# Lightning attention into a gated FFN: block 0's masks, k transposes and first outputs reordered, block 1's first transposes moved behind a gate

## The chip, the cores and the metric

One core of one Trainium2 chip. The metric is the device time of one execution in microseconds. All runs here were of the fast state, at a granted clock of 0.998 to 1.0, but for two executions at 0.992. A profile covers a span about 2.1 us shorter than that time (224.5 of 226.6 us for the kernel before).

## The reference

Causal linear attention with decay over blocks, then a gated FFN. Shapes: q, k, v (4, 8, 768, 64), d_model 512, d_ff 1536, float32 in and out.

```python
for b in range(nb):                                   # blocks along the sequence
    intra = einsum('bhic,bhjc->bhij', qb, kb) * Dmask # scores, decay mask
    intra = einsum('bhij,bhjd->bhid', intra, vb)      # output within the block
    inter = einsum('bhid,bhde->bhie', qb * lam_pow, kv_state)
    out[:, :, sl] = intra + inter
    kv_state = lam_block * kv_state + einsum('bhsd,bhse->bhde', kb * rev_pow, vb)
# x: (3072, 512)
gate = 1 / (1 + exp(-(x @ w_gate))); val = x @ w_val
return gate * val @ w_out
```

## The kernel before

It works in six blocks of 128 positions, all four batches (b0 to b3) together. In block 0 there is no state yet: q and k are turned on the matrix engine (PE), q is scaled (QS), k is copied (KS), scores (`piece_s`) are multiplied by a mask on the vector engine (DVE, `piece_m` gives MT), and MT times V gives the output (`piece_a0`), which the scalar engine (ACT) copies to XT. The FFN runs in 12 units of 128 columns, each a gate product, a value product and a multiplication; `gv(0, 8)` is unit 8 of block 0. While block 0's FFN runs, block 1's attention is slipped in between. All loads but those of q of b0 and b1 and of the decay factors go through Pool's queue in the order of the program.

The start, with cuts marked:

```python
    idle(10)                       # fillers: PE has nothing yet
    nc.vector.tensor_copy(Q[0][:, 0], q01[0])
    piece_tq0([0]); make_mask(0); idle(1)
    piece_tq0([1]); piece_tk0(0); make_mask(1); idle(1)
    piece_s(0, [0]); piece_m(0, 0); piece_s(0, [1]); piece_m(0, 1, (0,))
    piece_tk0(1)                   # k of b2, copy, k of b3, copy: one PSUM tile
    # ... (table load)
    piece_tq0([2]); piece_tq0([3]); piece_m(0, 1, (1,))
    piece_s(0, [2], ps_ff, "ff"); piece_m(0, 2)
    piece_s(0, [3]); piece_m(0, 3)
    make_kd0(0, nc.vector)         # decayed k for the state
    piece_a0(0); piece_a0(1); idle(2)
    piece_a0(2, (nc.scalar.copy, nc.scalar.copy))
    g0 = psum(); mm_part(g0, WG, 0, 0, 0, 3 * C)     # "first gate": b0 to b2
    v0 = psum(); mm_part(v0, WV, 0, 0, 0, 3 * C)
    piece_a0(3, (nc.scalar.copy, nc.vector.tensor_copy))
    make_kd0(1, nc.vector); c(0, 0)                  # state of b0, b1
    mm_part(g0, WG, 0, 0, 3 * C, TCH); sigm(0, 0, g0)   # "full gate": b3
    # ... unit 0's rest, unit 1, c(0, 1), units 2 to 8 ...
    gv(0, 8)
    t(1, 0)                        # turn q and k of block 1 (b0, b1), scale q, copy k
    gv(0, 9)
    sc(1, 0)                       # scores of block 1
```

Of the kernel before, what the change touches and what calls it, by code (L numbers as in the profile page):

```python
# [8 lines left out]
BF16 = mybir.dt.bfloat16  # L9
# [6 lines left out]
def kernel(  # L16
# [11 lines left out]
    nc = tc.nc  # L28

    B, H, S, D = q.shape  # L30
    C = 128
    NSTEP = S // C
    HP = H // 2
# [4 lines left out]
    TCH = B * C  # L38
# [5 lines left out]
    trsb = ctx.enter_context(tc.tile_pool(name="trsb", bufs=3))  # L44
# [6 lines left out]
    ps_at = ctx.enter_context(tc.tile_pool(name="ps_at", bufs=5, space=bass.MemoryType.PSUM))  # L51
    ps_ff = ctx.enter_context(tc.tile_pool(name="ps_ff", bufs=3, space=bass.MemoryType.PSUM))
# [8 lines left out]
    WG = const.tile([128, NMT, DFF], BF16, tag="WG")  # L61
    WV = const.tile([128, NMT, DFF], BF16, tag="WV")
# [5 lines left out]
    Q, K, V = {}, {}, {}  # L68
# [42 lines left out]
    nc.scalar.preload_act_table_set("natural_log_exp_and_others")  # L111
    ident = const.tile([128, 128], BF16, tag="ident")
    zero = const.tile([128, TCH], BF16, tag="zero")
    jn = const.tile([128, 2], FP32, tag="jn")
    ip1 = const.tile([128, C], FP32, tag="ip1")
    tri = const.tile([128, C], FP32, tag="tri")
    nc.vector.memset(zero, 0.0)
    Sb = stp.tile([128, B, HP, D], BF16, tag="Sb", name="Sb")
    nc.vector.memset(ip1[:, 0:1], 1.0)
    w = 1  # L120
# [30 lines left out]
    def idle(n):  # L151
        for i in range(n):
            nc.tensor.matmul(wm, lhsT=zero[:, :C], rhs=zero, start=True, stop=True,
                             skip_group_check=True)
# [40 lines left out]
    def make_mask(u):  # L195
        nc.vector.tensor_tensor(
            out=mask[:, u::2, :], in0=tri.unsqueeze(1).to_broadcast([128, HP, C]),
            in1=pk[:, u::2].unsqueeze(2).to_broadcast([128, HP, C]), op=ALU.mult)

    def masked(out, x, n, u):  # L200
        if n == 0:
            nc.vector.tensor_tensor(out=out, in0=x, in1=mask[:, u::2, :], op=ALU.mult)
            return
        nc.vector.tensor_tensor(  # L204
            out=out.rearrange("p (e x) c -> p e x c", e=2), in0=x.rearrange("p (e x) c -> p e x c", e=2),
            in1=mask.rearrange("p (x u e) c -> p u e x c", u=2, e=2)[:, u], op=ALU.mult)
# [7 lines left out]
    QS, KS, MT, XT, KD = {}, {}, {}, {}, {}  # L214

    QR, HB = {}, {}
# [20 lines left out]
    def transpose_pair(out, x, b, g):  # L237
        nc.tensor.transpose(out, x[:, b, 2 * g:2 * g + 2, :].rearrange("p h d -> p (h d)"), ident)  # L238

    def scale(n, bp, src):  # L240
        QS[n, bp] = trsb.tile([128, 2, 2, 2, C], BF16, tag="QS", name="QS")
        nc.vector.tensor_tensor(out=QS[n, bp].rearrange("p e i x c -> p e i (x c)"),
                                in0=src.rearrange("p e i x c -> p e i (x c)"),
                                in1=lamq_e.unsqueeze(2).to_broadcast([128, 2, 2, 2 * C]), op=ALU.mult)

    def piece_tq0(bs, then=None):
        tq = ps_at.tile([128, 2, 2, 2 * C], BF16, name="tq", tag="ps")
        for b in bs:
            if (0, b // 2) not in QS:
                QS[0, b // 2] = trsb.tile([128, 2, 2, 2, C], BF16, tag="QS", name="QS")  # L250
            for g in range(HP):
                transpose_pair(tq[:, b % 2, g // 2, g % 2 * C:g % 2 * C + C], Q[0], b, g)
        if then:
            then()
        for b in bs:
            nc.vector.tensor_tensor(out=QS[0, b // 2][:, :, b % 2].rearrange("p e x c -> p e (x c)"),
                                    in0=tq[:, b % 2], in1=lamq0_e, op=ALU.mult)

    def piece_tk0(bp):
        KS[0, bp] = trsb.tile([128, 2, 2, 2, C], BF16, tag="KS", name="KS")  # L260
        for i in range(2):
            if i == 0 or bp == 0:
                tk = ps_at.tile([128, 1 + bp, 2, 2 * C], BF16, name="tk", tag="ps")
            x = tk[:, i if bp else 0]
            for g in range(HP):
                transpose_pair(x[:, g // 2, g % 2 * C:g % 2 * C + C], K[0], 2 * bp + i, g)
            nc.scalar.copy(KS[0, bp][:, :, i].rearrange("p e x c -> p e (x c)"), x)  # L267

    def piece_t(n, bp):
        if n > 1 or bp == 1:  # L270
            scale(n, bp, QR[n][:, :, 2 * bp:2 * bp + 2] if n > 1 else HB["q"])
            return
        q1, k1 = (x[1][:, 0].rearrange("p (e b y d) -> p e b y d", e=2, b=2, y=HP) for x in (Q, K))
        tq = ps_at.tile([128, 2, 2, 2, C], BF16, name="tq", tag="ps")
        tk = ps_at.tile([128, 2, 2, 2, C], BF16, name="tk", tag="ps")

        def turn(out, x):
            for e in range(2):
                for i in range(2):
                    for g in range(2):  # L280
                        nc.tensor.transpose(out[:, e, i, g, :],
                                            x[:, e, i, 2 * g:2 * g + 2, :].rearrange("p y d -> p (y d)"), ident)

        turn(tq, q1)
        scale(n, bp, tq)
        turn(tk, k1)
        KS[n, bp] = trsb.tile([128, 2, 2, 2, C], BF16, tag="KS", name="KS")
        nc.scalar.copy(KS[n, bp], tk)

    SP = {}  # L290

    def piece_s(n, bs, pool=ps_at, tag="ps"):

        for b in bs:
            bp, i = b // 2, b % 2
            sp = [pool.tile([128, HP, C], FP32, name=f"sp{u}", tag=tag) for u in range(2)]
            for hp in range(HP):
                for u in range(2):
                    us = slice(u * 64, (u + 1) * 64)
                    nc.tensor.matmul(sp[u][:, hp, :], lhsT=KS[n, bp][us, hp // 2, i, hp % 2, :],  # L300
                                     rhs=QS[n, bp][us, hp // 2, i, hp % 2, :],
                                     start=(hp == 0), stop=(hp == HP - 1), skip_group_check=True)
            SP[n, b] = sp

    def piece_m(n, b, us=(0, 1)):
        if us[0] == 0:
            MT[n, b] = mtp.tile([128, 2, HP, C], BF16, tag="MT", name="MT")
        for u in us:
            masked(MT[n, b][:, u], SP[n, b][u], n, u)
# [32 lines left out]
    def piece_a0(b, split=()):  # L342
        if 0 not in XT:
            XT[0] = xtp.tile([128, NMT, B, C], BF16, tag="XT", name="XT")
        w = 2 if split else NMT
        for m0 in range(0, NMT, w):
            pool, tag = (ps_ff, "ff") if b == 2 and m0 else (ps_at, "ps")
            op = pool.tile([128, w, C], FP32, name="op", tag=tag)
            for m in range(w):
                intra(0, b, op[:, m, :], m0 + m, m == 0, m == w - 1)  # L350
            cp = split[m0 // w] if split else nc.scalar.copy
            cp(XT[0][:, m0:m0 + w, b, :], op)  # L352
# [78 lines left out]
    def mm_part(ps, W, n, ft, lo, hi):  # L431
        x = XT[n].rearrange("p m b c -> p m (b c)")
        for mt in range(NMT):
            nc.tensor.matmul(ps[:, lo:hi], lhsT=W[:, mt, ft * 128:(ft + 1) * 128], rhs=x[:, mt, lo:hi],  # L434
                             start=(mt == 0), stop=(mt == NMT - 1))

    def psum():
        return ps_ff.tile([128, TCH], FP32, name="gp", tag="ff")

    def sigm(n, ft, gp):  # L440
        HT[n, ft] = htp.tile([128, TCH], BF16, tag="sg", name="sg", bufs=3)
        nc.scalar.activation(HT[n, ft], gp, AF.Sigmoid)

    def prod(n, ft, vp):
        sg = HT[n, ft]
        HT[n, ft] = htp.tile([128, TCH], BF16, tag="ht", name="ht", bufs=2 * NFT)
        nc.vector.tensor_mul(HT[n, ft], sg, vp)
# [52 lines left out]
    nc.vector.tensor_copy(Q[0][:, 0], q01[0])  # L500
    piece_tq0([0])
    make_mask(0)
    idle(1)
    piece_tq0([1])
    piece_tk0(0)
    make_mask(1)
    idle(1)
    piece_s(0, [0])
    piece_m(0, 0)
    piece_s(0, [1])  # L510
    piece_m(0, 1, (0,))
    piece_tk0(1)
    nc.scalar.preload_act_table_set("sigmoid_and_others")
    piece_tq0([2])
    piece_tq0([3])
    piece_m(0, 1, (1,))
    piece_s(0, [2], ps_ff, "ff")
    piece_m(0, 2)
    piece_s(0, [3])
    piece_m(0, 3)  # L520
    make_kd0(0, nc.vector)
    piece_a0(0)
    piece_a0(1)
    idle(2)
    piece_a0(2, (nc.scalar.copy, nc.scalar.copy))
    g0 = psum()
    mm_part(g0, WG, 0, 0, 0, 3 * C)
# [18 lines left out]
    def t(n, bp):  # L546
        piece_t(n, bp)

    def sc(n, bp):
        piece_s(n, [2 * bp, 2 * bp + 1])  # L550
        piece_m(n, 2 * bp)
# [7 lines left out]
    def gv(n, *fts):  # L559
        for ft in fts:  # L560
            piece_gv(n, ft)
# [36 lines left out]
    lamq_end()  # L598
    gv(0, 6, 7)
    gv(0, 8)  # L600
    t(1, 0)
    gv(0, 9)
    sc(1, 0)
    m(1, 0)
    gv(0, 10)
# [101 lines left out]
```

## Time and profile before

| | |
|---|---|
| time, three runs | 226.60 us (226.56 to 226.66) |
| PE idle, 0 to 20 us | 3.8 of 20.0 us |
| PE idle, 20 to 191 us | 0.04 us |
| DMA engines busy, 5.6 to 40 us | 90% or more in every slice of the page |

PE's order is the kernel's time: from 20 us to the tail it never waits by the view of waits, so whatever starts it earlier ends the kernel earlier, unless something else is late. (That view misses stalls that the modelled ends of matmuls cover.) And the DMA engines are busy without a break in the stretch where PE starts. The sums come from the view of busy time by stretches (PE busy 3.81 + 2.17 + 2.71 + 3.62 + 3.90 in 0 to 20 us).

### The profile page before, as it was taken

The page shows a single profiled execution, that of the slowest core. Times are in us where ns is not written, and L with a number is a line of the kernel's source. Part 1 is how long each engine was busy: PE and PEld are TensorE (multiplying, and loading weights), DVE is VectorE, ACT ScalarE, POOL GpSimd, SP SyncE. Part 2 cuts the span into 40 slices and gives each one's busy share as a digit, 9 for nine tenths or more (in the row PEclk, how much of TensorE's full clock was granted, in tenths as well). Part 3 has the DMA queues.
Part 4 walks back from the last instruction along what each step waited for, and adds up shares of the span by engine and source line. Part 5 has one row for each costly group of instructions (what it writes and reads, how often), then busy time and mean ns, then how long its engine had stood idle before and what let it go on. Part 6 is the DMA issues. An engine that isn't in the chain of part 4 may idle for free.

```text
span 224.5 us, 4262 instructions
## 1 busy us (share of the span) xinstructions
PE 217.8 (97%) x1746; PEld 114.7 (51%) x1746; DVE 105.8 (47%) x192; ACT 79.8 (36%) x151; POOL 79.2 (35%) x78
## 2 busy tenths in 40 slices
PE   7689999999999999999999999999999999999994
PEld 2454455888854454444445444446444445444443
DVE  7797747595521713336732445742335840333300
ACT  5564334435422234333225333115333225333221
POOL 8996698983592008930006940000000000000000
PEclk9999999999999999999999999999999999999999
DMA  6999999999999992999021999021930012100022
GB/s 109 155 169 193 191 176 155 163 183 168 157 162 159 225 236 86 210 157 101 1 96 55 231 151 128 0 96 47 168 70 0 0 52 91 47 3 0 0 93 95
DMA packets 106419, 25.70 MB, mean 114 GB/s; under 512 B 97056, under 2 KB 103456, under 8 KB 106400
## 3 DMA queue, kind: packets, MB, share of 16 engines
q0 software_dynamic: 81792, 13.90, 81.6%
q1 hardware_dynamic: 23568, 11.28, 20.4%
q10 hardware_dynamic: 1040, 0.26, 0.5%
q8 instruction: 13, 0.21, 0.4%
q14 instruction: 6, 0.05, 0.1%
HBM read 28.32 MB, written 6.29 MB: 154 GB/s over the span
## 4 chain that ended last, share of the span: by engine, by line
PE 94%; DMA 3%; ACT 1%; issue 1%; DVE 0%; POOLq 0%
PE po L483 27%; PE gp L420 21%; PE vp L426 21%; PE gp L455 5%; PE gp L434 5%; PE vp L461 5%; PE sp L300 3%; PE op L313 3%; DMA kb<-in_k_dram 3%; PE op L325 1%; PE po L472 1%; PE cp L404 1%; ACT KS L267 1%; PE tk L238 1%; ACT XT L352 0%
## 5 line engine op out<-in xcount | busy, mean ns | idle before, releaser
L429 DVE TENSOR_TENSOR ht<-sg,vp 128x512 bf16<-128x512 bf16 x54 | 37.1, 687 | 64.2 <-PE vp L426 64.0
L483 PE MATMUL po<-WO,ht 128*128 128x512 bf16 x276 | 62.0, 379 | 0.0
L420 PE MATMUL gp<-XT,WG 128*128 128x512 bf16 x216 | 55.5, 379 | 0.0
L426 PE MATMUL vp<-XT,WV 128*128 128x512 bf16 x216 | 55.4, 379 | 0.0
L423 ACT ACTIVATE sg<-gp 128x512 bf16<-128x512 f32 x54 | 32.2, 597 | 59.0 <-PE gp L420 59.0
L483 PEld LDWEIGHTS <-ht 128*128 128x128 bf16 x276 | 26.3, 98 | 31.0
L426 PEld LDWEIGHTS <-WV 128*128 128x128 bf16 x216 | 21.2, 98 | 25.5
L420 PEld LDWEIGHTS <-WG 128*128 128x128 bf16 x216 | 20.8, 98 | 24.7
L486 ACT COPY ob<-po 128x512 f32<-128x512 f32 x23 | 13.5, 586 | 52.2 <-PE po L483 50.4
L204 DVE TENSOR_TENSOR MT<-sp,mask 128x512 bf16<-128x512 f32 x40 | 25.1, 682 | 9.1 <-PE sp L300 9.1
L382 POOL TENSOR_TENSOR sd<-Sb,dec 128x512 f32<-128x512 bf16 x8 | 8.1, 1037 | 41.2 <-DVE Sb L411 41.1
L455 PE MATMUL gp<-XT,WG 128*128 128x256 bf16 x96 | 14.4, 273 | 0.0
L461 PE MATMUL vp<-XT,WV 128*128 128x256 bf16 x96 | 14.4, 273 | 0.0
L465 DVE TENSOR_TENSOR ht<-sg,vp 128x256 bf16<-128x256 bf16 x24 | 10.0, 420 | 8.6 <-PE vp L461 8.6
L458 ACT ACTIVATE sg<-gp 128x256 bf16<-128x256 f32 x24 | 9.2, 384 | 13.0 <-PE gp L455 11.8
L91 POOL DMA_DIRECT2D vb<-in_v_dram x10 | 12.7, 1278 | 1.0 <-DMA WG<-in_moe_w_gate_dram 0.6
L373 POOL TENSOR_TENSOR kd<-kb,kds 128x1024 bf16<-128x1024 bf16 x6 | 11.3, 1904 | 4.7 <-PE vp L461 4.7
L411 DVE TENSOR_TENSOR Sb<-cp,sd 128x512 bf16<-128x512 f32 x8 | 5.2, 686 | 15.5 <-PE cp L404 15.5
L340 ACT CAST XT<-op 128x512 bf16<-128x512 f32 x19 | 9.9, 598 | 2.1 <-PE op L313 2.0
L455 PEld LDWEIGHTS <-WG 128*128 128x128 bf16 x96 | 9.2, 98 | 1.7 <-issue 0.2
L461 PEld LDWEIGHTS <-WV 128*128 128x128 bf16 x96 | 9.4, 98 | 1.1
L77 POOL DMA_DIRECT2D qb<-in_q_dram x8 | 9.4, 1182 | 0.0
(79 smaller groups left out, 162.1 us busy)
## 6 DMA issues: line engine op xcount, KB each, us to landing
out_dram<-ob SPq DMA_DIRECT2D x21, 256.0 KB, 2.0
kb<-in_k_dram POOLq DMA_DIRECT2D x10, 256.0 KB, 8.4
qb<-in_q_dram POOLq DMA_DIRECT2D x8, 256.0 KB, 8.1
vb<-in_v_dram POOLq DMA_DIRECT2D x4, 512.0 KB, 13.7
WO<-in_moe_w_out_dram POOLq DMA_DIRECT2D x3, 512.0 KB, 8.7
WV<-in_moe_w_val_dram POOLq DMA_DIRECT2D x5, 256.0 KB, 8.8
WG<-in_moe_w_gate_dram POOLq DMA_DIRECT2D x4, 256.0 KB, 8.6
qb<-in_q_dram POOLq DMA_DIRECT2D x6, 128.0 KB, 8.3
```

The costliest lines, as they stand in the source:

```text
L91: nc.gpsimd.dma_start(out=lst[n][:, b0:b1], in_=src[b0:b1, :, sl, :].rearrange("b h s d -> s (b h) d"))
L204: nc.vector.tensor_tensor(out=out.rearrange("p (e x) c -> p e x c", e=2), in0=x.rearrange("p (e x) c -> p e x c", e=2), in1=mask.rearrange ...
L373: nc.gpsimd.tensor_tensor(out=KD[n][:, e], in0=K[n][:, e], in1=kds[:, e::2].unsqueeze(1).unsqueeze(3).to_broadcast([128, B, HP, D]), op=AL ...
L420: nc.tensor.matmul(gp, lhsT=WG[:, mt, fs], rhs=x[:, mt, :], start=(mt == 0), stop=(mt == NMT - 1))
L423: nc.scalar.activation(sg, gp, AF.Sigmoid)
L426: nc.tensor.matmul(vp, lhsT=WV[:, mt, fs], rhs=x[:, mt, :], start=(mt == 0), stop=(mt == NMT - 1))
L429: nc.vector.tensor_mul(HT[n, ft], sg, vp)
L434: nc.tensor.matmul(ps[:, lo:hi], lhsT=W[:, mt, ft * 128:(ft + 1) * 128], rhs=x[:, mt, lo:hi], start=(mt == 0), stop=(mt == NMT - 1))
L455: nc.tensor.matmul(gp[:, cs], lhsT=WG[:, mt, fs], rhs=x[:, mt, cs], start=(mt == 0), stop=(mt == NMT - 1))
L461: nc.tensor.matmul(vp[:, cs], lhsT=WV[:, mt, fs], rhs=x[:, mt, cs], start=(mt == 0), stop=(mt == NMT - 1))
L483: nc.tensor.matmul(po, lhsT=HT[n, ft][:, tt * 128:(tt + 1) * 128], rhs=WO[:, ft, :], start=(ft == 0), stop=(ft == NFT - 1))
L486: nc.scalar.copy(ob, po)
```

## The change

Its intent: shorten the way from k's landing to the first FFN product by giving DVE a better order and taking a wait out of k's transposes; put b0's and b1's outputs in PE's pauses; and turn block 1's k later, when it has surely landed.

```diff
-    def piece_tk0(bp): # transposes of one batch, its copy, then the next, in one tile
+    def piece_tk0(*bs):
+        ...
+        for j, b in enumerate(bs):        # all transposes
+            ...
+        for j, b in enumerate(bs):        # then all copies
+            nc.scalar.copy(KS[0, bp]..., tk[:, j])
@@ start
     make_mask(0)
+    make_mask(1)
     idle(1)
     piece_tq0([1])
     piece_tk0(0)
-    make_mask(1)
+    piece_tk0(1)
 ...
-    piece_tk0(1)
+    piece_tk0(2, 3)
     piece_tq0([2])
-    piece_tq0([3])
     piece_m(0, 1, (1,))
-    piece_s(0, [2], ps_ff, "ff")
-    piece_m(0, 2)
+    def first():
+        piece_s(0, [2], ps_ff, "ff")
+        piece_m(0, 2, (0,))
+    piece_tq0([3], first)                 # first() before q of b3 is scaled
+    piece_m(0, 2, (1,))
+    piece_a0(0)
+    piece_a0(1)
     piece_s(0, [3])
     piece_m(0, 3)
     make_kd0(0, nc.vector)
-    piece_a0(0)
-    piece_a0(1)
-    idle(2)
     piece_a0(2, (nc.scalar.copy, nc.scalar.copy))
@@ block 1
-    t(1, 0)
-    gv(0, 9)
+    g9 = psum(); mm_part(g9, WG, 0, 9, 0, TCH); sigm(0, 9, g9)
+    scale(1, 0, turn(Q, (0, 1)))
+    for e, cp in enumerate((nc.scalar.copy, nc.vector.tensor_copy)):
+        cp(KS[1, 0][:, e:e + 1], turn(K, (e,)))   # half on ACT, half on DVE
+    v9 = psum(); mm_part(v9, WV, 0, 9, 0, TCH); prod(0, 9, v9)
```

(The zero memset also moves up past three tile declarations.)

More of the change, by code (lines that the diff above doesn't have):

```diff
@@ L113 @@
     zero = const.tile([128, TCH], BF16, tag="zero")
+    nc.vector.memset(zero, 0.0)
     jn = const.tile([128, 2], FP32, tag="jn")
@@ L116 @@
     tri = const.tile([128, C], FP32, tag="tri")
-    nc.vector.memset(zero, 0.0)
     Sb = stp.tile([128, B, HP, D], BF16, tag="Sb", name="Sb")
@@ L257, in piece_tq0 @@
                                     in0=tq[:, b % 2], in1=lamq0_e, op=ALU.mult)
-    def piece_tk0(bp):
-        KS[0, bp] = trsb.tile([128, 2, 2, 2, C], BF16, tag="KS", name="KS")
-        for i in range(2):
-            if i == 0 or bp == 0:
-                tk = ps_at.tile([128, 1 + bp, 2, 2 * C], BF16, name="tk", tag="ps")
-            x = tk[:, i if bp else 0]
+    def piece_tk0(*bs):
+        bp = bs[0] // 2
+        if (0, bp) not in KS:
+            KS[0, bp] = trsb.tile([128, 2, 2, 2, C], BF16, tag="KS", name="KS")
+        tk = ps_at.tile([128, len(bs), 2, 2 * C], BF16, name="tk", tag="ps")
+        for j, b in enumerate(bs):
@@ L265, in piece_tk0 @@
             for g in range(HP):
-                transpose_pair(x[:, g // 2, g % 2 * C:g % 2 * C + C], K[0], 2 * bp + i, g)
-            nc.scalar.copy(KS[0, bp][:, :, i].rearrange("p e x c -> p e (x c)"), x)
+                transpose_pair(tk[:, j, g // 2, g % 2 * C:g % 2 * C + C], K[0], b, g)
+        for j, b in enumerate(bs):
+            nc.scalar.copy(KS[0, bp][:, :, b % 2].rearrange("p e x c -> p e (x c)"), tk[:, j])
     def piece_t(n, bp):
-        if n > 1 or bp == 1:
-            scale(n, bp, QR[n][:, :, 2 * bp:2 * bp + 2] if n > 1 else HB["q"])
-            return
@@ L273, in piece_t @@
-        q1, k1 = (x[1][:, 0].rearrange("p (e b y d) -> p e b y d", e=2, b=2, y=HP) for x in (Q, K))
-        tq = ps_at.tile([128, 2, 2, 2, C], BF16, name="tq", tag="ps")
-        tk = ps_at.tile([128, 2, 2, 2, C], BF16, name="tk", tag="ps")
-        def turn(out, x):
-            for e in range(2):
-                for i in range(2):
-                    for g in range(2):
-                        nc.tensor.transpose(out[:, e, i, g, :],
-                                            x[:, e, i, 2 * g:2 * g + 2, :].rearrange("p y d -> p (y d)"), ident)
@@ L284, in piece_t, with turn @@
-        turn(tq, q1)
-        scale(n, bp, tq)
-        turn(tk, k1)
-        KS[n, bp] = trsb.tile([128, 2, 2, 2, C], BF16, tag="KS", name="KS")
-        nc.scalar.copy(KS[n, bp], tk)
+        scale(n, bp, QR[n][:, :, 2 * bp:2 * bp + 2] if n > 1 else HB["q"])
+    def turn(x, es):
+        x = x[1][:, 0].rearrange("p (e b y d) -> p e b y d", e=2, b=2, y=HP)
+        out = ps_at.tile([128, len(es), 2, 2, C], BF16, name="tq", tag="ps")
+        for j, e in enumerate(es):
+            for i in range(2):
+                for g in range(2):
+                    nc.tensor.transpose(out[:, j, i, g, :],
+                                        x[:, e, i, 2 * g:2 * g + 2, :].rearrange("p y d -> p (y d)"), ident)
+        return out
@@ L600 @@
     gv(0, 8)
-    t(1, 0)
-    gv(0, 9)
+    g9 = psum()
+    mm_part(g9, WG, 0, 9, 0, TCH)
+    sigm(0, 9, g9)
+    scale(1, 0, turn(Q, (0, 1)))
+    KS[1, 0] = trsb.tile([128, 2, 2, 2, C], BF16, tag="KS", name="KS")
+    for e, cp in enumerate((nc.scalar.copy, nc.vector.tensor_copy)):
+        cp(KS[1, 0][:, e:e + 1], turn(K, (e,)))
+    v9 = psum()
+    mm_part(v9, WV, 0, 9, 0, TCH)
+    prod(0, 9, v9)
     sc(1, 0)
```

## The prediction

> **What bounds the kernel now.** I read the page first: which engine fills the span?
>
> ```profile
> PE 217.8 (97%) x1746; PEld 114.7 (51%) x1746; DVE 105.8 (47%) x192; ACT 79.8 (36%) x151; POOL 79.2 (35%) x78
> PE 94%; DMA 3%; ACT 1%; issue 1%; DVE 0%; POOLq 0%
> ```
>
> The matrix engine (PE) is busy for 217.8 of 224.5 us. The program adds no arithmetic and takes away almost none, so only PE's idle time, 6.7 us, is there to win. The view of PE's waits lists where it lies:
>
> ```profile
> PE wm L153 <- DVE ip L119: 1.2, 1, 1.2
> PE tk L238 <- ACT KS L267: 0.7, 1, 0.7
> PE tk L238 <- DMA kb<-in_k_dram: 0.5, 1, 0.5
> PE gp L434 <- ACT XT L352: 0.3, 1, 0.3
> PE sp L300 <- DVE QS L256: 0.3, 1, 0.3
> ```
>
> All of these are in the first 17 us; from 20 us on the same view, asked for 20 to 45 us, gives no wait. About 3 us more is the tail (the last stretch, 191 to 224.5 us, has 30.64 us of PE in 33.50), which the change doesn't touch. So the question is when block 0 lets PE into the dense part. The chain of work, asked for the first 20 us, answers:
>
> ```profile
> 11.18 0.44 DVE QS L256
> 11.66 0.73 PE sp L300 x16
> 12.39 0.65 PE op L313 x16
> 13.04 0.54 PE wm L153 x2
> ...
> 14.09 0.38 ACT XT L352
> 14.51 1.46 PE gp L434 x8
> 15.97 0.25 PE op L313 x4
> 16.24 0.38 ACT XT L352
> 16.67 2.39 PE gp L434 x16
> ```
>
> The reader is to see the two places that matter: the first gate at 14.51, behind the copy (XT) of b2's output, and 16.67, behind the copy of b3's output; from there PE hardly stops. What the chain doesn't say is how close the loads are behind it. The timeline of the weight loads does:
>
> ```profile
> 13.51 0.11 PEld L313 LDWEIGHTS <-vb 128*64 128x64 bf16 x2 [0.42 <-DMA vb<-in_v_dram]
> 13.78 0.22 PEld L313 LDWEIGHTS <-vb 128*64 128x64 bf16 x6 [0.16 <-issue]
> 14.23 0.10 PEld L434 LDWEIGHTS <-WG 128*128 128x128 bf16 x1 [0.23 <-DMA WG<-in_moe_w_gate_dram]
> 15.90 0.25 PEld L313 LDWEIGHTS <-vb 128*64 128x64 bf16 x8 [0.32 <-DMA vb<-in_v_dram]
> 32.28 0.22 PEld L281 LDWEIGHTS <-kb 128*128 128x128 bf16 x4 [0.17 <-DMA kb<-in_k_dram]
> ```
>
> V of b2, the first gate weights and V of b3 land only just ahead of their use. In the trace's own landing times: V 11.75, 12.58, 13.45 and 15.75 us for b0 to b3, WG 14.19, first WV 14.91; block 1's second half of k lands at 32.24. The last line is a PE stall that the waits view misses, since modelled matmul ends cover it.
>
> **What the Trainium skill says.** "DMA: Bandwidth & Descriptors", Anatomy of one DMA: DMA engines do not wait on semaphores, the issuing sequencer does. The trace agrees: Pool issues the loads one after another from 1.26 to 12.0 us without a pause and waits for no compute engine, so reordering compute can't move the landings. "PSUM — Partial Sum Buffer", PSUM bank collisions: accesses of two engines to one bank must be kept apart by semaphores, by bank and not by address. The trace agrees with that form: the transposes of b3's k write the other half of a tile that ACT is reading, and wait for it (0.7 us above). "TensorE: Matmul & The Clock Gate", Back-to-back issue gap: N/2.4 + 2.5 ns, so 56 ns for 128 columns and 216 for 512; the trace has those steps, and I use them to find hidden stalls. Part 1 of that page: an idle window of about 3.4 us halves PE's clock. The trace shows the slow start (the first ten fillers 427 ns apart, later ones 216-226), and no return to it.
>
> **The change part by part.**
>
> 1. The zero memset moves up past tile declarations, which emit nothing: 0. Both orders have it as DVE's first instruction (0.86 us).
>
> 2. The second mask (0.68 us on DVE) goes ahead of the second scaled q (0.42). Now they run 7.34 to 8.35 in the other order. The second q would end near 8.4 instead of 7.75; the scores that need it start at 9.13, the masks' first use is at 9.08. Both keep slack: 0.
>
> 3. K of b2 and b3: all eight transposes, then two copies. PE's 0.7 us wait disappears; by 8 x 56 ns the transposes run 9.46 to 9.91 instead of to 10.75. Then q of b2 (landed 10.04) can turn at 10.09 and its scaling follows the third masked product at once, at 10.88 instead of 11.18, in place of DVE's 0.21 us pause plus its start-up. This **0.30 us** is what part 4 can use.
>
> 4. DVE's new order from there, by spacings of the trace (0.34 for a scaled q, 0.60 for a masked product): q2 at 10.88, b1's second product 11.22, b2's first 11.82, q3 12.42, b2's second 12.76 to 13.44. The scores of b2 can start at 11.36 and are ready near 11.8, in time. Before, b2's second product ended at 13.72, so b2's output, which began at 13.51, had to pause until 13.78. Now the pause goes, but V of b2 (13.45) doesn't come earlier: the output starts at 13.50, its copy begins 0.34 later (as b3's does: 15.90 to 16.24), takes 0.37, and the gate starts at 14.26, just after WG's 14.23. **0.25 us** earlier than 14.51, near the floor.
>  PE then does four gate matmuls (4 x 0.162 = 0.65) to 14.95 when WV has just landed, four more to 15.6, and waits for V of b3, landed 15.75, so usable at 15.80. It began this step at 15.90. So of the 0.25 us only **0.10 us** gets through; 0.15 turns into a wait for V. The remaining path (output, copy, 16.67) shifts with it, to 16.56.
>  The outputs of b0 and b1 between the scores go to 11.8 and 12.63, behind their V; the more frequent switches between 64-row scores, narrow outputs and full tiles cost some 0.09 us each (12.17 to 12.32 where one 56 ns step was due), all inside waits. The two fillers removed (0.43 us of PE) stood in a wait as well: 0.
>
> 5. Block 1's transposes behind unit 9's gate (4 x 216 = 0.86 us). Now the fifth k transpose starts at 32.288, 219 ns after the fourth instead of 56: **0.16 us** of stall for the load that landed at 32.24. After the move, k is turned from about 32.66 on, past the landing, even with PE 0.10 earlier. The 0.16 goes, and the 0.10 of part 4, which this same landing would otherwise eat, is kept.
>  The price is time to the scores: v9's matmuls (0.86) are now the only work between k's transposes and them, from 33.11 to 33.97. ACT's half copy (some 0.59 by block 0's 128x512) runs 33.07 to 33.66; DVE scales q to about 33.5 and copies the other half (estimate 0.42, as its 128x512 operations of 16-bit data) to 33.9. Scores at 34.07 instead of 34.34; first needed is ACT's half. It fits with 0.1 us to spare.
>
> Sum: 0.10 + 0.16 = **0.27 us**. After 35 us I looked at every pair of neighbouring matmuls for a step longer than its columns ask: besides the fixed 0.09 at tile switches only 40.39 (0.14, a product on DVE) and 52.38 (0.20, a sigmoid on ACT) show. Both hang on PE's own earlier work and shift along; the last load in reach, WV of units 10 and 11, lands at 35.19, against its weight load now near 35.29. So nothing gives the gain back.
>
> **The rivals.** (a) **The loads hide block 0's part altogether.** If V of b3 or WV comes 0.1 us later by chance, part 4 yields 0 and only 0.16 stays: 226.44. For it speaks that three landings lie within 0.15 us of their uses. (b) **A new wait for block 1's k copies** on DVE or ACT: one in-order queue holds unit 8's product, the scaled q, the copy. If the copy ends 0.3 us later than I have it, the scores wait 0.2 and the total is 226.5. Against it: DVE was idle for over a microsecond before each product there. (c) **PE falls to half clock** because the fillers are gone. Gaps of PE between 9.9 and 14.2 would be at most 0.6 us each, far from 3.4, but useful work is thin. One window at half rate would cost up to 1.7 us: 228. Against it: the stretch from 9.3 to 11.7 was as thin before and stayed fast. (d) **The whole 0.7 us plus 0.43 us come through**: PE time is freed, and a reader of shares would say 225.5. Against it: V's landing at 15.75.
>
> **Range and chances.** From 226.60 us take 0.27: 226.33 us. Rivals (a) and (b) reach 226.5 and the spread of the three runs is 0.1, so the upper end is 226.58; landings 0.1 us earlier and another 0.1 from smaller waits give the lower end, 226.08. A change of 2% is 4.5 us, and no rival reaches it: the whole idle time of PE outside the tail and the start is under 3 us. Faster by over 2%: 0.005; within 2%: 0.985; slower: 0.01, kept for rival (c) repeated.
>
> **What would show each step.** Right: no wait of a k transpose for ACT's copy; first gate near 14.26 and a load wait for V ahead of b3's output near 15.80; the full gate resuming near 16.56; no load wait at block 1's k; scores of block 1 near 34.07. Wrong: landings of V moved by more than 0.1 us; the scores of block 1 waiting for the copies; fillers' step of 427 ns for full matmuls after 14 us; or a stall after 35 us that takes the 0.27 us back.

## The result, and the profile after

| | before | changed |
|---|---|---|
| median of 6 runs | 226.58 us | 226.33 us |
| lowest to highest | 226.24 to 226.69 | 226.22 to 226.40 |
| span of the profile | 224.5 | 224.2 |

Ratios are those of fast runs, with their 95% intervals; they aren't quite the ratios of the medians. The first was 0.9991 (0.9978 to 1.0003), by itself not clear of noise; two later sets of the changed kernel gave 0.998 (0.9963 to 0.9996) and 0.9985 (0.9972 to 0.9997), with medians of 226.36 and 226.31. Over all sets, 33 executions of the kernel before have a median of 226.60 us and 17 of the changed one 226.35. So a gain of about 0.25 us is real. It isn't the same in every execution: seven of before's 33 took 226.21 to 226.36, as little as the changed kernel's (226.16 to 226.41).

The view of PE's waits of the changed kernel (us in total, times, longest):

```profile
PE tk L238 <- DMA kb<-in_k_dram: 0.5, 1, 0.5
PE tq L238 <- DMA qb<-in_q_dram: 0.4, 1, 0.4
PE op L306 <- DMA vb<-in_v_dram: 0.4, 1, 0.4
PE gp L427 <- ACT XT L345: 0.4, 1, 0.4
```

The wait of a k transpose for ACT's copy (0.7 us) is gone. In its place stand waits for loads: q of b3, then V (of b1, at 12.60). The chain of work, from 13 us on, now begins with a load:

```profile
7.23 6.17 DMA vb<-in_v_dram
...
13.44 0.32 PE op L306 x4
...
13.79 0.38 ACT XT L345
...
14.21 1.53 PE gp L427 x8
...
15.76 0.32 PE op L306 x4
...
16.53 2.39 PE gp L427 x16
```

The first gate moved from 14.51 to 14.21, the full gate only from 16.67 to 16.53. The weight loads say why (start, length, and in brackets the idle time before and what ended it):

```profile
13.44 0.25 PEld L306 LDWEIGHTS <-vb 128*64 128x64 bf16 x8 [0.28 <-DMA vb<-in_v_dram]
14.92 0.44 PEld L427 LDWEIGHTS <-WV 128*128 128x128 bf16 x4 [0.27 <-DMA WV<-in_moe_w_val_dram]
15.76 0.25 PEld L306 LDWEIGHTS <-vb 128*64 128x64 bf16 x8 [0.40 <-DMA vb<-in_v_dram]
32.58 0.49 PEld L279 LDWEIGHTS <-kb 128*128 128x128 bf16 x8
```

The outputs of b2 and b3 and unit 0's value product now start 0.04 us after their load lands: V at 13.40 and 15.72, the value weights at 14.88. The two gates follow the copies of those outputs. The eight k transposes of block 1 run without a break. What the vector engine did with its time, before and then changed:

```profile
11.18 0.76 DVE L256 TENSOR_TENSOR QS<-tq,lamq 128x512 bf16<-128x512 bf16 x2 [0.21 <-PE tq L238]
11.85 3.07 DVE L202 TENSOR_TENSOR MT<-sp,mask 128x512 bf16<-128x512 f32 x5
```
```profile
10.85 0.42 DVE L256 TENSOR_TENSOR QS<-tq,lamq 128x512 bf16<-128x512 bf16 x1
11.18 1.28 DVE L202 TENSOR_TENSOR MT<-sp,mask 128x512 bf16<-128x512 f32 x2
```

The scaled q of b2 follows at once at 10.85, with no bracket: the idle 0.21 us is gone. So far the prediction's mechanism stands. But one thing in this profile was not foreseen: block 1's second half of k landed at 31.51 us, against 32.24 in the profile of before, though nothing about loads was changed. If k lands that early, block 1's part of the change has nothing to gain. That made the experiments necessary.

### The profile page after: what moved, and what is told of

It is laid out like the page before. It is cut to its first block, busy times and chain, and to the rows that moved or that the text cites. A ratio compares the mean times of both kernels' runs of the same rounds, so it can differ in the third digit from the quotient of the medians.

```text
span 224.2 us, 4261 instructions
## 1 busy us (share of the span) xinstructions
PE 217.6 (97%) x1744; PEld 114.3 (51%) x1744; DVE 105.9 (47%) x193; ACT 79.5 (35%) x151; POOL 79.2 (35%) x78
## 4 chain that ended last, share of the span: by engine, by line
PE 92%; DMA 3%; POOL 3%; issue 0%; ACT 0%; DVE 0%; POOLq 0%
PE po L476 27%; PE gp L413 21%; PE vp L419 20%; PE gp L427 6%; PE gp L448 5%; PE vp L454 5%; DMA vb<-in_v_dram 3%; PE op L306 3%; PE sp L293 2%; PE op L318 1%; PE po L465 1%; POOL kb L91 1%; PE cp L397 1%; POOL qb L91 1%; POOL vb L91 1%
## 5 line engine op out<-in xcount | busy, mean ns | idle before, releaser
L422 DVE TENSOR_TENSOR ht<-sg,vp 128x512 bf16<-128x512 bf16 x53 | 36.5, 688 | 62.6 <-PE vp L419 62.5
L413 PE MATMUL gp<-XT,WG 128*128 128x512 bf16 x212 | 54.4, 379 | 0.0
L419 PE MATMUL vp<-XT,WV 128*128 128x512 bf16 x212 | 54.4, 379 | 0.0
L416 ACT ACTIVATE sg<-gp 128x512 bf16<-128x512 f32 x53 | 31.6, 597 | 59.3 <-PE gp L413 59.3
L419 PEld LDWEIGHTS <-WV 128*128 128x128 bf16 x212 | 20.7, 98 | 25.0
L454 PEld LDWEIGHTS <-WV 128*128 128x128 bf16 x96 | 9.4, 98 | 1.1
```

The source lines that it names most:

```text
L413: nc.tensor.matmul(gp, lhsT=WG[:, mt, fs], rhs=x[:, mt, :], start=(mt == 0), stop=(mt == NMT - 1))
L416: nc.scalar.activation(sg, gp, AF.Sigmoid)
L419: nc.tensor.matmul(vp, lhsT=WV[:, mt, fs], rhs=x[:, mt, :], start=(mt == 0), stop=(mt == NMT - 1))
L422: nc.vector.tensor_mul(HT[n, ft], sg, vp)
L454: nc.tensor.matmul(vp[:, cs], lhsT=WV[:, mt, fs], rhs=x[:, mt, cs], start=(mt == 0), stop=(mt == NMT - 1))
```

## The experiments

All kernels gave correct results. "Before" stands for 27 more executions of it in these sets.

### Each part alone, and both kernels again

The edits: `blk0_only` is the changed kernel with block 1's part undone, `blk1_only` the kernel before with that part alone; the other two are the same programs again.

```diff
 # blk0_only, against the changed kernel
-    g9 = psum(); ...; v9 = psum(); mm_part(v9, ...); prod(0, 9, v9)
+    t(1, 0)
+    gv(0, 9)
```

> Block 0's parts alone (masks, transposes, first outputs, fillers), block 1 as before. Theory (two separate stalls, the k landing fixed at 32.24 us): the first 17 us gain 0.14 us, full gate resumes near 16.53, but the fifth k transpose of block 1 still begins at 32.29, so the whole 0.14 is eaten there: time equal to before, 226.58. Rival (the k landing moves with the order of the start, as it was 31.51 us in the changed kernel's profile): no stall at the k transposes and a gain of 0.14 + 0.16 = 0.30 us, as much as the full change.

> Block 1's part alone (its first q and k turned behind unit 9's gate), block 0 as before. Theory: first 17 us as before (full gate resumes at 16.67), the 0.16 us stall at the fifth k transpose goes, scores of block 1 near 34.18 instead of 34.34: 226.42. Rival: if k lands near 31.5 in this program too, the part is worth nothing and the gain would show without it.

> The changed kernel once more, on this chip beside the others. Both theories: 226.33, first gate 14.21, full gate resumes 16.53, block 1's scores 34.03. Where block 1's second half of k lands tells whether 31.51 us belongs to the program (again within 0.1) or to the execution (anywhere from 31.5 to 32.3).

> The kernel before once more, with a profile of its own. Both theories: ratio 1.000, time 226.58. Theory: block 1's second half of k lands at 32.24 again, with a 0.16 us step at the fifth k transpose. Rival: it lands elsewhere (31.5 to 32.3), since the loads' landing differs from execution to execution; then the stall is only in part of the executions and before's spread of 226.24 to 226.69 comes from it.

Times: `blk0_only` 226.58 us (226.50 to 227.26), ratio 0.9995; `blk1_only` 226.67 (226.24 to 227.19), 0.9994; `after_again` 226.36 (226.20 to 226.40), 0.998; `before_again` 226.56 (226.25 to 227.22), 0.9998. Neither part alone lowers the median. For block 0's part the profile shows why; in `blk1_only` three slow executions of six spoil the median, and `tk_split`, below, shows what block 1's part is worth. First `blk0_only`, then `before_again`, the weight loads of block 1's k:

```profile
32.18 0.23 PEld L282 LDWEIGHTS <-kb 128*128 128x128 bf16 x4 [0.31 <-DMA kb<-in_k_dram]
```
```profile
31.77 0.49 PEld L282 LDWEIGHTS <-kb 128*128 128x128 bf16 x8
```

With block 0 faster, PE reaches k earlier and waits longer: the step to the fifth transpose is 0.30 us over its due, against 0.16 in before. Block 1's scores come 2.10 us after k's landing in both (34.243 after 32.140; 34.344 after 32.242), so what block 0 had won is eaten whole, as the first theory had it. (The theory put that gain at 0.14; by the table below it is 0.05 in this execution, and the rest of the longer stall comes from the landings.) But `before_again` has no stall at all: there k landed at 31.55. So where k lands belongs to the execution, not to the program, and the rival was right on that (its claim that k's landing follows from block 0's order fell: `blk0_only` had 32.14, `after_again` 32.29).

In `blk1_only` something else shows, in PE's timeline:

```profile
18.52 1.04 PE L426 MATMUL gp<-XT,WV 128*128 128x512 bf16 x4 [0.55 <-DMA WV<-in_moe_w_val_dram]
```

Unit 1's value weights landed at 18.47 instead of 17.0 to 17.4 and cost 0.71 us beyond the due step. That execution took 226.98 us, and half of `blk1_only`'s six were over 226.9. The other three took 226.24 to 226.37, as the changed kernel does; none of them has a profile.

**Block 0 in numbers.** Times of the trace, in us, K being the landing of k of b0 and b1, V that of V of b3:

| program | K | V | first gate | full gate | after K | after V |
|---|---|---|---|---|---|---|
| before | 7.525 | 15.750 | 14.509 | 16.666 | 9.141 | 0.916 |
| before_again | 7.447 | 15.673 | 14.435 | 16.593 | 9.146 | 0.920 |
| blk1_only | 7.300 | 15.570 | 14.285 | 16.443 | 9.143 | 0.873 |
| changed | 7.490 | 15.717 | 14.210 | 16.528 | 9.038 | 0.811 |
| after_again | 7.305 | 15.590 | 14.065 | 16.402 | 9.097 | 0.812 |
| blk0_only | 7.316 | 15.594 | 14.065 | 16.406 | 9.090 | 0.812 |

The old order resumes 9.14 us after K, wherever V is: it is bound by the work that follows k. The new order resumes 0.81 us after V, wherever K is: it is bound by the load. The gain is what lies between, 0.05 to 0.105 us.

### What inside block 0 does it

`tk_split` lets b3's k transposes wait for b2's copy again; `slack_back` puts the second mask behind the second scaled q and the fillers ahead of b2's output.

```diff
 # tk_split, against the changed kernel
-    piece_tk0(2, 3)
+    piece_tk0_split()   # b2's transposes, its copy, b3's transposes, its copy
 # slack_back, against the changed kernel
-    make_mask(1)                        # moved behind piece_tk0(1)
+    idle(2)                             # ahead of piece_a0(2, ...)
```

> The changed kernel, but b3's k transposes again wait for the copy of b2's k in the same tile. Theory (the removed wait is what lets the vector engine start 0.30 us earlier, and 0.14 of it passes V's landing): the wait of 0.7 us is back, the scaled q of b2 starts near 11.2 instead of 10.85, the first gate near 14.5 and the full gate near 16.65 (against V of b3 landing 15.7): block 0's gain is gone, the time 0.1 to 0.15 us above the changed kernel. Rival (the earlier outputs and the mask order carry the gain): the first gate stays near 14.2.

> The changed kernel with the old order of the second mask (behind the second scaled q and k's copies) and with the two fillers back ahead of b2's output. Theory: both stand in slack; the second mask again ends before the first masked product begins at 9.04; the fillers, now behind b3's scores at about 13.2, push b2's output from 13.44 to about 13.75, the first gate to 14.5, but V of b3 absorbs all but 0.1 us of it. So mask order 0, fillers 0 to 0.14 us. Rival (fillers hold the clock): no step of 427 ns for a full matmul in either.

`tk_split`: 226.36 us (226.35 to 226.49), ratio 0.9989. Its view of PE's waits has the wait back:

```profile
PE tk L238 <- ACT KS L276: 0.7, 1, 0.7
```

The scaled q of b2 starts at 10.97 (10.67 in `early_fetch`, an execution with the same K of 7.31), the first gate at 14.30, and the full gate at 16.456, which is 9.144 us after K: the old figure to 5 ns. So this one wait is all that separates the old block 0 from the new; the order of the outputs and the masks adds nothing by itself. The time didn't rise by the 0.1 us expected, though, because later loads decide in part (below).

This run also settles which part carries the gain. With block 0 as slow as before (9.144 us) but block 1's part in, the time is 226.36 us, that of the changed kernel; with block 0's part alone it is 226.58, that of before. So block 1's part carries the visible gain, and `slack_back` below, with block 0 slower still, says the same. Block 0's part adds at most its 0.05 to 0.1 us, where no later load waits.

`slack_back`: 226.40 us (226.38 to 226.41), ratio 0.9989. The first masked product begins 1.55 us after K with either mask order (8.855 - 7.305 here, 9.042 - 7.490 in the changed kernel): mask order 0. The fillers, in PE's timeline (one of the two has no record):

```profile
13.37 0.38 PE L153 MATMUL wm<-zero 128*128 128x512 bf16 x1 [0.16 <-issue]
13.68 0.41 PE L306 MATMUL op<-MT,vb 128*64 128x128 bf16 x8
```

They push b2's output to 13.68 and the full gate to 1.008 us after V, 0.20 later than the changed kernel's 0.811, more than the 0.14 I had allowed. In the new order b3's scores already fill that pause, so the fillers must go. Full matmuls run 216 ns apart with and without them, so they didn't hold the clock here.

### Why the loads land differently

From the full gate to block 1's scores the trace has 17.506 us in `before_again`, 17.507 in the changed kernel and 17.506 in `tk_split`: PE's own work. Where it is longer, the long steps stand at loads. From the scores to the end it is 190.13 to 190.17 us in twelve of the fourteen profiles (190.25 in `tk_split`, 190.28 in `after_plus4`). So nearly all of the difference between these kernels arises before 34 us, as full gate + 17.51 + load stalls:

| program | k of block 1 landed | values of units 4, 5 landed | over 17.506 | scores |
|---|---|---|---|---|
| before | 32.24 | 23.50 | 0.172 | 34.344 |
| before_again | 31.55 | 22.81 | 0 | 34.099 |
| blk0_only | 32.14 | 23.39 | 0.331 | 34.243 |
| changed | 31.51 | 22.77 | 0 | 34.035 |
| after_again | 32.29 | 23.54 | 0.176 | 34.084 |
| after_third | 32.22 | 23.46 | 0.114 | 34.005 |

In this table there are two kinds of execution, 0.7 us apart in the loads that land between 19 and 34 us. Of all fourteen profiles three have this k at 31.51 to 31.55 and nine at 32.14 to 32.34; `c01_early` (31.68) and `before_nofill` (31.95) lie between. `after_again` shows that the changed kernel also stalls in the late kind, not at k but mostly at the value weights of unit 4:

```profile
23.58 0.33 PEld L428 LDWEIGHTS <-WV 128*128 128x128 bf16 x3 [0.43 <-DMA WV<-in_moe_w_val_dram]
```

What moves the loads? The page's DMA part has a queue named instruction, with 13 packets of 16 KB on q8. The packet records place the first between 15.8 and 17.0 us in every profile, when PE has issued 268 to 313 weight loads and matmuls, and it takes about 0.9 us where the loads' packets there take 0.04. The Trainium skill ("Runtime: NRT & Kernel Launch", Terms) says that each engine's instruction memory is refilled in 16 KiB blocks; 13 such blocks fit PE's 3,490 or so instructions at some 270 each, and `early_fetch` below, with 40 more, has 14; that these packets are PE's is inferred from that. The DMA view of the changed kernel, 16 to 18 us (packets, MB, and the sum of their times as a share of 16 engines' time):

```profile
q0 software_dynamic: 1360, 0.35, 176.6%
q8 instruction: 1, 0.02, 2.8%
```

One packet, in the middle of the loads. To see whether it delays them, `early_fetch` makes 40 PE instructions more in the start, in place of four large fillers, so that the fetch should come sooner:

```diff
-    idle(10)
+    idle(6)
+    for i in range(24): nc.tensor.matmul(wm[:32, :64], lhsT=zero[:, :32], rhs=zero[:, :64], ...)
```

> The changed kernel with 40 more PE instructions (20 more pairs, smaller fillers) in the start, where PE waits anyway. Theory (loads' landings differ between executions because a 16 KB fetch of PE's instructions, the first near PE instruction 270, sits in one DMA engine's way for 0.9 us): the fetch moves from 16.7 to about 15 us, V of b3 or the loads just after it land up to 0.8 us later, the full gate resumes near 17.3 in part of the executions, and the time is 0.2 to 0.8 us longer with a wider spread. Rival (plain jitter of the loads): time as the changed kernel, 226.35, landing of V of b3 at 15.6 to 15.75.

227.17 us (226.45 to 227.22), ratio to before 1.0014 (1.0001 to 1.0027). The fetch came at 15.81, and unit 1's gate weights landed at 17.83 where the other profiles have 16.3 to 16.5; V of b3 (15.60) was already safe. PE's view of waits has a new line:

```profile
PE gp L427 <- DMA WG<-in_moe_w_gate_dram: 0.8, 1, 0.8
```

So more PE instructions in the start, and with them an earlier fetch, cost 0.8 us in the median against the changed kernel. But the time of the fetch alone doesn't decide: in `before_again` it came at 16.29 and unit 1's value weights landed at 17.17, undisturbed, while in `blk1_only` it came at 16.42 and they landed at 18.47. One thing goes with the kinds of execution in all fourteen profiles: the first fetch took 893 ns in the five with k at or before 31.95, and 935 to 974 ns in the nine others. Why, no run tells. Two more kernels asked whether it also explains the executions over 226.9 us, 7 of before's 33 in all sets:

```diff
 # before_nofill, against the kernel before
-    idle(2)
 # after_plus4, against the changed kernel
+    for i in range(2): nc.tensor.matmul(wm[:32, :64], ...)     # after idle(10)
```

> The kernel before without its two fillers ahead of b2's output: four PE instructions fewer before 16 us, nothing else. Block 0's timing theory: the fillers lie in a wait, the full gate still resumes 9.14 us after k of b0 and b1 lands. Fetch theory (the slow executions of before, 226.9 us and over, are those in which PE's first instruction fetch, at PE instruction 270 or so, starts before unit 1's value weights have landed; four instructions fewer move it behind PE's wait for the copy of b3's output): fetch at 16.65 or later and no execution over 226.85, median 226.5. Rival (chance): as before, about a quarter of the executions over 226.9.

> The changed kernel with two tiny filler pairs more at the very start: four PE instructions more before 16 us, no PE time on the path. Fetch theory: some executions at 226.7 to 227.2, with the first fetch at 16.2 to 16.5 and unit 1's value weights landing near 18.4. Rival (chance): 226.2 to 226.4 like the changed kernel's 12 executions so far.

> The changed kernel a third time, for the spread and as the neighbour of the other three: both theories 226.2 to 226.4, and no execution over 226.85.

`after_plus4`: 226.70 us, three of six executions at 227.02 to 227.25 and three at 226.30 to 226.37, as the fetch theory had it. The kept profile is of one of the fast three (fetch at 16.67, unit 1's value weights at 17.00), so where the fetch stood in the slow ones isn't known. `after_third`: 226.31 us (226.16 to 226.41); none of the changed kernel's 17 executions is over 226.41. But `before_nofill`: 226.62 us (226.27 to 227.71), with the fetch at 16.35, unit 1's value weights at 18.47 and two executions over 226.9. Four instructions fewer did not free the kernel before, so that half of the theory fell. That four instructions more bring slow executions to the changed kernel is shown; why the kernel before has them with and without its fillers, and why its one sibling with the new start, `blk0_only`, had one (227.26), stays open. Counted over all sets, the kernels with the old start (before, `before_nofill`, `blk1_only`) had 12 of 45 executions over 226.9 us, those with the new one (leaving out `early_fetch` and `after_plus4`) 1 of 40: a gain of the change that the prediction didn't have. The fillers' own time was as expected, 0: the full gate came 9.147 us after K.

### A version that beats both

After V's landing PE still waits 0.27 us for the copy of b3's output. The second state product, `c(0, 1)`, with its two tile switches, stands behind unit 1. To put it in that wait, its decayed k must be ready: b0's is made in DVE's pause before the first masked product, the rest behind the last.

```diff
     piece_tk0(1)
+    make_kd0(0, 1)        # b0
 ...
-    make_kd0(0, nc.vector)
+    make_kd0(1, 3); make_kd0(3, 4)
 ...
-    make_kd0(1, nc.vector); c(0, 0)
+    c(0, 0, 1)
 ...
-    c(0, 1); keep(1)      # behind unit 1
+    keep(1)
```

> The changed kernel with block 0's second state product moved into PE's wait for the copy of b3's output; for that the decayed k of b0 is made in the vector engine's pause before 9.04 and the rest behind the masked products. Theory (PE's order after V of b3's landing is what is left to win): full gate 0.07 later (16.6), but 0.25 us of matmuls and two tile switches of 0.09 are gone behind unit 1, so unit 2's gate starts 0.36 us earlier. Where k lands late (32.2), the loads of units 4 and 5 and of k take 0.1 to 0.3 of it back: 226.0 to 226.3. Rival (the loads after 17 us are already the limit): no gain, 226.35.

> The version with the second state product in PE's wait, once more beside the changed kernel on one chip. Theory: 225.7 to 226.15, the scores of block 1 0.3 us earlier than the changed kernel's, less what the loads take back.

`c01_early`: 225.96 us (225.69 to 226.15), ratio 0.9973 (0.9959 to 0.9986); `c01_again`: 225.96 us (225.93 to 225.99), 0.997 (0.9956 to 0.9983), beside 226.31 of the changed kernel in the same set. PE's timeline of `c01_early`:

```profile
15.89 0.76 PE L397 MATMUL cp<-vb,kd 128*64 128x64 bf16 x32
16.58 0.40 PE L427 MATMUL gp<-XT,WG 128*128 128x128 bf16 x4
```

The full gate came 0.977 us after V, so 0.17 later than the changed kernel's 0.811 and not 0.07: the last decayed k was ready at 16.27, and PE paused 0.06 us for it. But full gate to scores took 17.178 us instead of 17.507, 0.33 less. In `c01_again` loads were late, and the scores stood at 10.542 us after unit 4's values, the same as `after_again`'s 10.542 and `after_third`'s 10.543: this version too runs into that load.

## Why the prediction was right

It gave 226.33 us and 226.33 was measured. The exact hit is luck: the two parts, 0.10 and 0.16 us, were found at about these sizes, but in different kinds of execution, and don't simply add up. Step by step:

- **The bound and the stretch** were right: nearly all of the difference arises before 34 us.
- **Parts 1 and 2, memset and mask: 0.** The mask is confirmed by `slack_back`; the memset shows no change in PE's start.
- **Part 3, 0.30 us on DVE.** The scaled q of b2 begins 3.653 us after K before and 3.355 after: 0.298. `tk_split` shows that it alone carries block 0's gain.
- **Part 4, 0.25 us at the first gate, 0.10 through.** Measured against K: 6.984 to 6.720, so 0.264, and 9.141 to 9.038, so 0.103. V's landing absorbs the rest. In executions where V lands 8.28 us after K instead of 8.23, only 0.05 comes through. The fillers' removal is free only as part of the old order (`before_nofill`); put back into the new one they cost 0.20.
- **Part 5, 0.16 us at block 1's k.** Right where k lands late (before, `blk0_only`), zero where it lands early (`before_again`, changed). The prediction took the landings of one profile for those of the kernel; rival (a) let them differ by 0.1 us, and they differ by 0.7. The copies never delayed block 1's scores: the step ahead of them is over its due by the 0.096 us of the tile switch, before and after. So rival (b) did not come. By `tk_split`, this part is what the median gained.
- **"Nothing gives the gain back"** is where it erred. I looked for long steps after 35 us only. In the late kind of execution the changed kernel meets unit 4's value weights at 23.5 us and loses 0.11 to 0.18, most of it there, more than the 0.05 that block 0's part had won in those executions.
- **"Reordering compute can't move the landings"** doesn't hold for changes in the number of PE instructions: 40 more of them in `early_fetch` moved a landing from 16.3 to 17.83.
- **The sum** is therefore an average that fits, not a figure that holds in each execution. Early kind: spans of 224.256 (`before_again`) and 224.191, 0.065 us, which is 0.108 against K less 0.043 of later K. Late kind: before's scores stand 10.85 us after unit 4's values landed, the changed kernel's 10.54, so 0.31 us. 0.27 lies between. The early kind's gain is block 0's part, the late kind's nearly all block 1's: `tk_split`, in the late kind, has its scores at 33.962, no later than the changed kernel's 34.005 and 34.084.
- **Rivals (c) and (d)** did not come: full matmuls kept to 216 ns, and the freed 0.7 + 0.43 us of PE became waits for loads. (On those 216 ns: the section "Back-to-back issue gap" that the prediction cites gives its formula for an isolated matmul, and for pairs of weight load and matmul 81 ns at 128 columns and 131 at 512; the pairs here ran at 56 and 216.)

## What to carry to other kernels

Before you shorten a chain, set the landing times of the loads beside it: what it can gain is the way to the next landing, and the rest turns into a wait there (0.26 us became 0.10 here). A part that shows no gain by itself may be hidden by a few slow executions, as block 1's seems to have been, so take a part out of the whole as well as putting it in alone. And take landings from several executions, since one profile can be of either kind; a hole that stays open in all of them is the place for other ready work, as the last version shows.

## What the Trainium skill lacked or had wrong

- "DMA: Bandwidth & Descriptors", Queues, rings and completion order, names refill traffic as runtime-internal on row 14 and says that an engine drains a whole packet of one ring before it turns to the next; how long a refill packet is, and that it can hold up a kernel's own loads, it doesn't say. Here what we take for PE's instruction fetches are 16 KB packets on q8, 13 in all (8 KB ones on q14), 0.88 to 1.41 us each in the kernel before; with the first at 15.81 us, a weight load landed at 17.83 instead of 16.3 to 16.5.
- No page that I read says that the landings of one program differ between its executions; here by 0.7 to 0.8 us for loads between 19 and 34 us (31.51 and 32.29 for the same k of the changed kernel).
- "TensorEngine Tiling (Array Packing)", Key Properties, says that a change of tiling mode drains PE, without a figure; here the step at such a change is 0.09 to 0.10 us over its due (0.089 to 0.100), at every change after 34 us in the kernels before and changed.
